# AFNO block: a chunk's moves split between SyncE's and GpSimd's queue

## The chip, the core and the metric

The kernel runs on one core of a Trainium2 chip. A core has five engines that run side by side and meet through semaphores: TensorE (matmuls; PE in the profile), VectorE (DVE), ScalarE (ACT), GpSimd (POOL) and SyncE (SP), which here only issues DMAs. DMAs can be issued by SyncE, ScalarE or GpSimd. The metric is the device time of one launch in microseconds (us), the median of several executions.

## The reference

One transformer-like block on 4096 positions of 640 channels, in float32:

```python
mod = (silu(c) @ w_mod)            # six vectors of 640: sa, ca, ga, sb, cb, gb
h = layernorm(x) * (1 + ca) + sa
x = x + ga * AFNO(h)
h = layernorm(x) * (1 + cb) + sb
x = x + gb * ((silu(h @ w_gate) * (h @ w_up)) @ w_down)

def AFNO(x):                       # 4 blocks of 160 channels
    z = rfft2(x over positions)
    h = relu(z * w1 + b1)          # complex products, block by block; relu on real and imaginary part
    o = softshrink(h * w2 + b2, 0.01)
    return irfft2(o)
```

## The kernel before, in words

The Fourier transform over 4096 positions is factored as 128 x 32 and done by matmuls with constant matrices. The AFNO stage takes some 50 to 300 us of the run, the feed-forward layer the rest.

The frequencies are worked off in 8 **chunks** (`ch`), each of which has 4 blocks of channels (`b`). One pass of the main loop is one **slot**, numbered `p = 4*ch + b`. In a slot TensorE, VectorE and ScalarE work on several chunks at once, as in a pipeline written out by hand: the first layer of slot `p` (`stage_l1`), the second stage of the forward transform for a later block (`stage_b`, `evac_b`), the second layer of slot `p - 1` (`stage_l2`), soft shrinkage of an earlier tile in four steps (`shrink_parts`, `shrink`, `shrink_high`, `shrink_low`), and the first stage of the inverse transform (`stage_i`) of slot `p - 7`. The order in which these are written in the loop is the order in which each engine gets its instructions; there is no scheduler in this stage. Every float32 matmul operand is split into a high and a low part, so most steps exist twice.

What touches the change:

- `stage_l2` writes its result with VectorE (L709) into `tts[ch, q]`, `q` = 0 and 1: two tiles of 128 partitions with real and imaginary part (`r`) beside each other. There are two `tt` buffers in all, so chunk `ch + 1` writes over those of chunk `ch`. Each slot fills one block's columns of both tiles; the first addition of a slot is for `q` = 0, the second for `q` = 1.
- When a chunk's four blocks are done (in the slot with `b == 0` of the next chunk), `move_x` copies `tt` by DMA from SBUF to SBUF into four tiles `xx`, `i` = 0 to 3: tile `i` takes the partitions `64*(i % 2)` to `64*(i % 2) + 63` of `tts[ch, i // 2]`, the real part to its lower 64 partitions, the imaginary part to its upper 64. That is eight DMAs of 64 rows of 2,560 bytes. So tiles 0 and 1 come from `q` = 0, tiles 2 and 3 from `q` = 1. `xx` has five buffers: tile 3 gets the one that tile 2 of the chunk before held, and `shrink_low` of the same slot is its last reader.
- `xx` then goes through the shrinkage, one tile in each of the following slots; `stage_i` multiplies it by a constant matrix, ScalarE copies the product to a tile `co` (two buffers, L763), and GpSimd issues the DMA that writes it to DRAM (`s2`, L764; `s<-co` in the profile).
- Behind the moves, SyncE's program has the loads of the modulation weights (`mod_load`, L531, tile `wm`), which VectorE adds up in the next slot (`mod_add`, L536 and L538), the next chunk's input (`load_g`) and, after the moves of slot 28, the load of the first rows of `x` for the layer that follows (`load_first`, L886).

The last chunk (7) isn't moved; it is shrunk and transformed in place. So there are seven handovers, in slots 4, 8, ..., 28.

Of the kernel before, what the change touches and what calls it, by code (L numbers as in the profile page):

```python
# [173 lines left out]
def body(tc, x, w1, b1, w2, b2, wg, wu, wd, c, wm, k_fa, k_tb, k_tx, k_bm, k_bx, k_ga, k_ge, k_id, out, dbg=None):  # L174
    nc = tc.nc
    pe, act, dve, pool = nc.tensor, nc.scalar, nc.vector, nc.gpsimd
# [25 lines left out]
    with ExitStack() as top:  # L202
# [35 lines left out]
        with ExitStack() as af:  # L238
# [40 lines left out]
            def weights_high(w, h, l, v, sg, eng=None):  # L279
                if eng:  # L280
                    eng.tensor_scalar(w[:, :, h], v, sg, None, op0=OP.mult)
                else:
                    act.activation(w[:, :, h], v, AF.Copy if isinstance(sg, float) else AF.Identity, scale=sg)

            def weights_low(w, h, l, v, sg):
                dve.scalar_tensor_tensor(w[:, :, l], v, sg, f32(w[:, :, h]), op0=OP.mult, op1=OP.subtract)
# [9 lines left out]
            def load_tb(ch):  # L296
                tb = lp.tile([P, 4, 128], F32, tag="tb", bufs=2, name=f"tb{ch}")
                nc.sync.dma_start(tb, k_tb[:, 4 * ch:4 * ch + 4])
                tbs[ch] = tb


            def load_g(ch, us=None):
                if ch not in gs:
                    gs[ch] = fx.tile([P, 4, D], F32, tag="gx", bufs=2, name=f"g{ch}")
                f, e = (ch, 1) if ch < 2 else (2, 2) if ch < 4 else (3, 4)
                src = s1[f].rearrange("(u v) (q e j) d -> e u (v q) (j d)", u=4, e=e, q=4)[ch % e]
                if us is None:
                    nc.sync.dma_start(gs[ch].rearrange("p j d -> p (j d)"), src.rearrange("u r d -> r u d"))
                else:
                    for u in us:  # L310
                        nc.sync.dma_start(gs[ch][u:P:4].rearrange("p j d -> p (j d)"), src[u])
# [210 lines left out]
            w, h, l, v, _ = prep2[5]  # L522
# [62 lines left out]
            tts = {}  # L585
# [4 lines left out]
            def stage_b(ch, t, tag=None):  # L590
                g, tb = gs[ch], tbs[ch]
                pb = (ps.tile([P, 2, 256], F32, tag=tag, name=f"pb{ch}_{t}") if tag else
                      bank0(1 if t == 4 else 0, [P, 2, 256], f"pb{ch}_{t}"))
                col = slice(128 * t, 128 * t + 128)
                for j in range(4):
                    mm(pb[:, :, 64 * j:64 * j + 64], g[:, j, col], tb[:, j, :], start=True, stop=True)
                pbs[ch, t] = pb

            def evac_b(ch, t):
                pb = pbs[ch, t]  # L600
                z = lp.tile([P, 2, 2, 258], F32R, tag="z", bufs=4, name=f"z{ch}_{t}")
                zs[ch, t] = z
                act.activation(z[:, 0, :, 0:256], pb, AF.Identity, scale=ca1[:, t:t + 1])
                dve.scalar_tensor_tensor(z[:, 1, :, 0:256], pb, ca1[:, t:t + 1],
                                         f32(z[:, 0, :, 0:256]), op0=OP.mult, op1=OP.subtract)
                if ch == CE:
                    pool.tensor_copy(z[:, 0, :, 0:257:256], f32(edge[:, 0, t]))
                    pool.tensor_copy(z[:, 1, :, 0:257:256], f32(edge[:, 1, t]))
                    pool.tensor_copy(z[:, :, :, 257], zero[:, 0, 0])
# [106 lines left out]

            xxs = {}

            def move_x(ch, i):
                q, h = i // 2, i % 2  # L720
                xx = p2.tile([P, D], F32, tag="xx", bufs=5, name=f"xx{ch}_{i}")
                for r in range(2):
                    nc.sync.dma_start(xx[64 * r:64 * r + 64, :], tts[ch, q][64 * h:64 * h + 64, r, :])
                xxs[ch, i] = xx


# [92 lines left out]
            def load_first_rows(lo, hi, q, e=slice(0, D)):  # L819
                for k in range(2):  # L820
                    q.dma_start(cf[k][lo:hi, :, e], s2[lo:hi, 2 * k:2 * k + 2, e])
# [4 lines left out]
            for p in range(LAST + 1):  # L826
                ch, b = p // 4, p % 4
                on(shrink, p - 6)
                on(stage_l1, p)


                if p < 4:
                    todo = ([(0, 2)], [(0, 3)], [(1, 4), (1, 0)], [(1, 1)])[p]
                elif b == 0:
                    todo = [(ch, 3)]
                else:
                    todo = [(ch + 1, 4)] * (b == 1) + [(ch + 1, b - 1)]
                todo = [q for q in todo if q[0] < NCH]
                for q in todo:
                    stage_b(*q)  # L840
                    if q[1] < 4:
                        evac_b(*q)
                for f, *a in sums.get(p, ()):
                    f(*a)

                rows = [p + 2] * (p < 4) + [p + 3] * (p > 2)
                for k in rows:
                    on(evac_rh, k)
                on(tail_l1, p)
                on(shrink_high, p - 6)  # L850
                for k in rows:
                    on(evac_rl, k)
                on(tail_low, p)
                on(stage_l2, p - 1)
                if p == 3:
                    stage_b(1, 2)
                    evac_b(1, 2)
                on(stage_i, p - 7)
                on(shrink_low, p - 6)
                if p < LAST:  # L860
                    on(shrink_parts, p - 5)
                if b == 0 and ch:
                    for i in range(4):
                        move_x(ch - 1, i)
                if p == 0:
                    for n in (3, 4):
                        weights_high(*prep2[n])
                    for job in prep2[2:5]:
                        weights_low(*job)
                if p == 0:  # L870
                    pool.dma_start(bm.rearrange("p a b c -> p (a b c)"), k_bm)
                if p == 2 or b == 3 and 2 < ch + 2 < NCH:
                    load_g(ch + 2)
                    load_tb(ch + 2)
                for f, *a in mods.get(p, ()):
                    f(*a)
                if p == LAST - 4:
                    cf += [rp.tile([P, 2, D], F32, tag=tag, name=f"cf{tag}") for tag in ("rm", "rr")]
                    load_first_rows(rb + 16, rl, nc.sync)
                elif p == LAST - 1:  # L880
                    load_first_rows(0, rb - 16, nc.sync)
# [153 lines left out]
        with ExitStack() as ff:  # L1035
# [1081 lines left out]
            for t in range(NS):  # L2117
                for n in range(NW):
                    if sum_at(n) == t:
                        a, b = sum_w(n)  # L2120
# [69 lines left out]
```

## Time and profile before

| | us |
|---|---|
| median of 3 runs | 1467.93 |
| lowest, highest | 1465.82, 1468.88 |
| the profiled execution's own time | 1467.72 |
| its span from first to last instruction | 1465.9 |

The granted TensorE clock was 0.997 in the mean. In the profile's rows a timeline line has the start, the duration, the engine, the source line, the operation and its tiles, and in brackets the idle time before it with what ended that. In a table of windows, each engine has its busy time and the number of its instructions; the last three columns are the granted clock, the mean busy share of the 16 DMA engines, and the GB/s that they moved. An `SPq` row is SyncE issuing a DMA; "to landing" is from the start of the issue to the completion semaphore. The chain of work that ended last is followed back from the last instruction to whatever released each step.

### The profile page before, as it was taken

The page shows a single profiled execution, that of the slowest core. Times are in us where ns is not written, and L with a number is a line of the kernel's source. Part 1 is how long each engine was busy: PE and PEld are TensorE (multiplying, and loading weights), DVE is VectorE, ACT ScalarE, POOL GpSimd, SP SyncE. Part 2 cuts the span into 40 slices and gives each one's busy share as a digit, 9 for nine tenths or more (in the row PEclk, how much of TensorE's full clock was granted, in tenths as well). Part 3 has the DMA queues.
Part 4 walks back from the last instruction along what each step waited for, and adds up shares of the span by engine and source line. Part 5 has one row for each costly group of instructions (what it writes and reads, how often), then busy time and mean ns, then how long its engine had stood idle before and what let it go on. Part 6 is the DMA issues. An engine that isn't in the chain of part 4 may idle for free.

```text
span 1465.9 us, 23617 instructions
## 1 busy us (share of the span) xinstructions
PE 1424.5 (97%) x8626; PEld 1344.9 (92%) x8626; DVE 1058.7 (72%) x1893; ACT 780.8 (53%) x1514; POOL 420.8 (29%) x549
## 2 busy tenths in 40 slices
PE   7899999989999999999999999999999999999998
PEld 2699999868888888899999999999999999999998
DVE  8878888888877777667777677678665566465653
ACT  7779989645445455445545455445453344344331
POOL 5500200155545244222333422434311122011111
PEclk9999999999999999999999999999999999999999
DMA  9856556667677976795766996676974446844422
GB/s 378 309 198 208 172 184 214 211 192 230 227 257 258 329 264 224 276 357 180 259 228 221 337 318 198 220 240 207 357 264 130 143 128 223 324 141 149 139 76 83
DMA packets 155223, 331.73 MB, mean 226 GB/s; under 512 B 19969, under 2 KB 79169, under 8 KB 153090
## 3 DMA queue, kind: packets, MB, share of 16 engines
q1 hardware_dynamic: 146722, 313.66, 63.0%
q0 software_dynamic: 6800, 13.93, 3.0%
q10 hardware_dynamic: 1584, 2.62, 0.5%
q8 instruction: 68, 1.11, 0.3%
q14 instruction: 49, 0.40, 0.1%
HBM read 234.35 MB, written 86.31 MB: 219 GB/s over the span
## 4 chain that ended last, share of the span: by engine, by line
PE 69%; DMA 10%; DVE 9%; ACT 5%; issue 2%; POOL 2%; SPq 2%; DVEq 0%; POOLq 0%; ACTq 0%
PE pd L2063 23%; PE pw L1868 8%; PE pw L1870 7%; PE pw L1869 7%; PE pg L1791 3%; PE pg L1792 3%; PE pg L1793 3%; DMA cr<-s 3%; PE pw L1879 2%; PE pw L1880 2%; PE pw L1881 2%; PE pc L707 2%; DMA wdr<-in_B_w_down_dram 1%; DMA wt<-td 1%; PE py L1511 1%
## 5 line engine op out<-in xcount | busy, mean ns | idle before, releaser
L2063 PE MATMUL pd<-wdh,a 128*128 128x320 f32 x1672 | 381.5, 310 | 0.5 <-DVE x L2035 0.3
L2063 PEld LDWEIGHTS pd<-wdh,a 128*128 128x128 f32 x1672 | 283.0, 188 | 1.7 <-DVE x L2035 0.7
L2063 PE MATMUL pd<-wdl,a 128*128 128x320 f32 x868 | 267.4, 309 | 0.0
L2035 DVE TENSOR_TENSOR x<-x,pd 128x320 f32<-128x320 f32 x384 | 178.2, 481 | 94.9 <-PE pd L2063 92.1
L1325 DVE TENSOR_TENSOR wb<-r,wb 128x512 fp32r<-128x512 f32 (+3 forms) x170 | 170.3, 1008 | 16.2 <-ACT wb L1318 14.9
L2063 PEld LDWEIGHTS pd<-wdl,a 128*128 128x128 f32 x868 | 163.2, 188 | 0.5
L1868 PE MATMUL pw<-h,wt 128*128 128x384 f32 x416 | 141.1, 339 | 5.0 <-DMA wt<-td 2.3
L1422 ACT ACTIVATE wdh<-wdr 128x640 fp32r<-128x640 f32 x84 | 60.8, 733 | 158.5 <-PE pd L2063 146.3
L1870 PE MATMUL pw<-h,wt 128*128 128x384 f32 x416 | 139.7, 336 | 0.0
L1869 PE MATMUL pw<-h,wt 128*128 128x384 f32 x416 | 139.5, 335 | 0.0
L1318 ACT ACTIVATE wb<-r 128x768 fp32r<-128x768 f32 (+3 forms) x168 | 115.3, 701 | 20.3 <-PE pg L1793 11.5
L1912 POOL TENSOR_TENSOR sg<-s_x,sg 128x384 f32<-128x384 f32 x24 | 26.5, 1103 | 340.0 <-DVE s_x L1894 298.4
L1868 PE MATMUL pw<-h,wb 128*128 128x384 f32 x312 | 105.0, 337 | 0.0
L1870 PE MATMUL pw<-h,wb 128*128 128x384 f32 x312 | 104.6, 335 | 0.0
L1869 PE MATMUL pw<-h,wb 128*128 128x384 f32 x312 | 104.5, 335 | 0.0
L1791 PE MATMUL pg<-ht,wb 128*128 128x512 f32 x260 | 103.7, 399 | 0.0
L1915 DVE TENSOR_TENSOR a<-sg,a 128x384 fp32r<-128x384 f32 x104 | 79.6, 769 | 32.8 <-ACT a L1914 32.5
L1792 PE MATMUL pg<-ht,wb 128*128 128x512 f32 x260 | 102.0, 392 | 0.0
L1793 PE MATMUL pg<-ht,wb 128*128 128x512 f32 x260 | 101.8, 392 | 0.0
L1426 DVE TENSOR_TENSOR wdl<-wdr,wdh 128x640 fp32r<-128x640 f32 x84 | 75.9, 913 | 27.5 <-ACT wdh L1422 27.1
L1868 PEld LDWEIGHTS pw<-h,wt 128*128 128x128 f32 x416 | 78.0, 188 | 8.1 <-ACT s_y L1887 3.9
L1494 POOL TENSOR_TENSOR cr<-cr,gab 128x640 f32<-128x640 f32 x28 | 48.5, 1734 | 116.1 <-DMA cr<-s 99.0
(276 smaller groups left out, 3370.9 us busy)
## 6 DMA issues: line engine op xcount, KB each, us to landing
wt<-td SPq DMA_DIRECT2D x104, 512.0 KB, 5.2
hs<-ho SPq DMA_DIRECT2D x52, 512.0 KB, 5.7
h<-hs SPq DMA_DIRECT2D x32, 768.0 KB, 7.3
r<-in_B_w_up_dram SPq DMA_DIRECT2D x36, 640.0 KB, 4.8
r<-in_B_w_gate_dram SPq DMA_DIRECT2D x36, 640.0 KB, 4.6
wdr<-wdd SPq DMA_DIRECT2D x35, 640.0 KB, 4.6
td<-wt SPq DMA_DIRECT2D x25, 512.0 KB, 7.1
xx<-tt SPq DMA_DIRECT2D x56, 160.0 KB, 3.4
```

Source lines behind the costliest of these rows:

```text
L1318: def high(ks, e=slice(0, c), copy=lambda o, i: act.activation(o, i, AF.Copy)):
L1325: dve.tensor_tensor(wbs[t, n][:, 1, ks, e], raw[t, n][:, ks, e], f32(wbs[t, n][:, 0, ks, e]), op=OP.subtract)
L1426: dve.tensor_tensor(l[:, f], wdraw[t, p][:, f], f32(h[:, f]), op=OP.subtract)
L1791: mm(b, wh, hh, start=(kk == 0), stop=False)
L1792: mm(b, wh, hl, start=False, stop=False)
L1793: mm(b, wl, hh, start=False, stop=(kk == 4))
L1868: mm(b, w(0, kp), a[:, kp, 0], start=start and kp == 0, stop=False, skip_group_check=not start)
L1869: mm(b, w(0, kp), a[:, kp, 1], start=False, stop=False, skip_group_check=not start)
L1870: mm(b, w(1, kp), a[:, kp, 0], start=False, stop=kp == 1, skip_group_check=not start)
L1915: Step("V", cv_ + 0.1, lambda: dve.tensor_tensor(o[:, 1], sg, f32(o[:, 0]), op=OP.subtract), (("ah", key),), ("act", t, fc, a), free=("sg" ...
L2035: dve.tensor_tensor(x2[:, e], x2[:, e], x[0][:, :320], op=OP.add)
L2063: mm(pd[g, hf][0][:, :320], l, m, start=i == 0, stop=i == len(s) - 1 and not (last and len(gs) > 1))
```

## The change

`move_x` gets the issuing engine as an argument. Tiles 0 and 1 of a chunk are still issued by SyncE, tiles 2 and 3 by GpSimd. And the call of the four moves stands directly behind `stage_l2`, ahead of `stage_i`, `shrink_low` and `shrink_parts` of the slot.

```diff
-            def move_x(ch, i):
+            def move_x(ch, i, eng=nc.sync):
                 q, h = i // 2, i % 2
                 xx = p2.tile([P, D], F32, tag="xx", bufs=5, name=f"xx{ch}_{i}")
                 for r in range(2):
-                    nc.sync.dma_start(xx[64 * r:64 * r + 64, :], tts[ch, q][64 * h:64 * h + 64, r, :])
+                    eng.dma_start(xx[64 * r:64 * r + 64, :], tts[ch, q][64 * h:64 * h + 64, r, :])
                 xxs[ch, i] = xx
...
                 on(stage_l2, p - 1)
+                if b == 0 and ch:
+                    for i in range(4):
+                        move_x(ch - 1, i, pool if i > 1 else nc.sync)
                 if p == 3:
                     stage_b(1, 2)
                     evac_b(1, 2)
...
                 on(shrink_low, p - 6)
                 if p < LAST:
                     on(shrink_parts, p - 5)
-                if b == 0 and ch:
-                    for i in range(4):
-                        move_x(ch - 1, i)
```

## The prediction

> **What bounds the kernel now.** I read the page first (busy shares and the chain that ended last), then who waits for the moves, then one handover in the timeline, then the DMA engines while moves run.
>
> ```profile
> PE 1424.5 (97%) x8626; PEld 1344.9 (92%) x8626; DVE 1058.7 (72%) x1893; ACT 780.8 (53%) x1514; POOL 420.8 (29%) x549
> PE 69%; DMA 10%; DVE 9%; ACT 5%; issue 2%; POOL 2%; SPq 2%; DVEq 0%; POOLq 0%; ACTq 0%
> xx<-tt SPq DMA_DIRECT2D x56, 160.0 KB, 3.4
> ```
>
> TensorE is busy 97% of the span, so time comes back only where TensorE itself waits, or where the chain has left it. The 56 moves are seven handovers of eight (slots 4, 8, ... 28). Who waits for them is VectorE's addition into the next chunk's `tt` (L709), which may not overwrite a buffer that a move still reads. Its rows, idle time before each in brackets:
>
> ```profile
> 100.24 0.49 DVE L709 TENSOR_TENSOR tt<-pc,b2t 128x320 f32<-128x320 f32 x1 [1.22 <-DMA xx<-tt]
> 127.79 0.49 DVE L709 TENSOR_TENSOR tt<-pc,b2t 128x320 f32<-128x320 f32 x1 [2.00 <-DMA xx<-tt]
> 157.87 0.49 DVE L709 TENSOR_TENSOR tt<-pc,b2t 128x320 f32<-128x320 f32 x1 [1.99 <-DMA xx<-tt]
> 186.69 0.49 DVE L709 TENSOR_TENSOR tt<-pc,b2t 128x320 f32<-128x320 f32 x1 [1.52 <-DMA xx<-tt]
> 217.44 0.49 DVE L709 TENSOR_TENSOR tt<-pc,b2t 128x320 f32<-128x320 f32 x1 [0.70 <-DMA xx<-tt]
> 247.38 0.49 DVE L709 TENSOR_TENSOR tt<-pc,b2t 128x320 f32<-128x320 f32 x1 [2.20 <-PE pl L670]
> 277.11 0.49 DVE L709 TENSOR_TENSOR tt<-pc,b2t 128x320 f32<-128x320 f32 x1 [1.02 <-PE pl L657]
> ```
>
> Seven waits, one at each handover, 10.65 us together. The last two name TensorE as releaser; the chain below shows moves landing just then (243.62 + 3.63, 272.74 + 4.25), so I count them as waits for moves. Each is before the second addition of its slot, the one that needs `tt[ch, 1]`: exactly the half that the change puts on another queue. What of this TensorE feels is much less:
>
> ```profile
> 131.91 0.42 PE L760 MATMUL pi<-xh,bm 128*128 128x320 f32 x1 [1.05 <-DVE u L675]
> 187.45 0.63 PE L657 MATMUL pl<-z,w1a 128*128 128x258 f32 x3 [1.02 <-DVE tt L715]
> 251.24 0.41 PE L760 MATMUL pi<-xh,bm 128*128 128x320 f32 x1 [0.25 <-DVE u L675]
> 268.38 0.41 PE L761 MATMUL pi<-xl,bm 128*128 128x320 f32 x1 [1.04 <-DVE xl L749]
> ```
>
> The first three follow the handovers of slots 8, 16 and 24: 2.32 us. The waits at 157.87 and 217.44 reach TensorE not at all. So 2 us, not 10, is the natural size of the prize.
>
> **Why a handover takes so long.** Slot 8, with the moves' landing from the chain:
>
> ```profile
> 118.89 6.00 SPq L723 DMA_DIRECT2D xx<-tt  x8
> 124.99 5.18 SPq L531 DMA_DIRECT2D wm<-in_w_mod_dram  x2
> 119.01 0.54 POOL L764 DMA_DIRECT2D s<-co  x1 [6.40 <-ACT co L763]
> 119.17 0.81 DVE L749 TENSOR_TENSOR xl<-xx,xh 128x640 fp32r<-128x640 f32 x1
> 125.29 0.49 DVE L709 TENSOR_TENSOR tt<-pc,b2t 128x320 f32<-128x320 f32 x1
> ...
> 124.29 3.41 DMA xx<-tt
> 243.62 3.63 DMA xx<-tt
> 272.74 4.25 DMA xx<-tt
> ```
>
> SyncE needs 6.00 us to issue eight moves, and the last lands at 127.70, 8.81 us after the first issue. The issue looks like the limit. But the windows over the moves (the last two columns are DMA share and GB/s) say that the DMA engines are full:
>
> ```profile
> 120.00:127.70 7.70, 7.70 (x64) 7.70 (x63) 5.28 (x10) 7.58 (x18) 0.54 (x1) 1.00 0.95 252
> 121.00:122.00 1.00, 1.00 (x10) 1.00 (x9) 1.00 (x3) 0.98 (x4) 0.00 (x0) 1.00 1.00 320
> ...
> s<-co POOLq DMA_DIRECT2D x28, 320.0 KB, 3.7
> wm<-in_w_mod_dram SPq DMA_DIRECT2D x20, 320.0 KB, 3.0
> x<-in_A_x_dram SPq DMA_DIRECT2D x1, 1280.0 KB, 8.7
> ```
>
> Ahead of the last landing lie eight moves of 160 KB and the 320 KB of `s<-co`, issued at 119.01: 1.64 MB, at 252 GB/s 6.5 us. The remaining 8.81 - 6.5 = 2.3 us are start and completion. So faster issue alone brings little; what counts is which bytes stand ahead of the second half.
>
> **The change part by part.** *Moved to GpSimd's queue*: 28 of the 56 moves, four in each handover. The instruction order of the two built kernels shows four fewer on SyncE, four more on GpSimd, the rest of SyncE's order as it was, and unchanged orders on TensorE, VectorE and ScalarE. GpSimd's price for issuing, from its other DMAs:
>
> ```profile
> L316 POOL DMA_DIRECT2D g<-xa x4: 572/584/797, 47.9 to 50.2; - x4
> DMA to landing us min/median/max: 3.4/3.6/4.0
> ...
> L764 POOL DMA_DIRECT2D s<-co x28: 539/542/591, 112.0 to 293.9; - x28
> ```
>
> L316 is SBUF to SBUF, as the moves are: 4 x 0.58 = 2.3 us. The two on the first tile can start when the second addition of slot 8 ends (about 119.3). The two on the last tile reuse the buffer that `shrink_low` (L749) still reads, to 119.98; SyncE had the same wait, but reached it late. The last issue starts near 121.2, against 124.29 before. GpSimd is otherwise idle here (6.40 us before L764), so the issue itself is hidden.
>
> *Placed behind the second layer*: on SyncE nothing lies between the old place and the new, so there this moves nothing. On GpSimd the four moves pass the same slot's write `s<-co`, which leaves some 2 to 3 us later and behind 640 KB. Cover: `co` has two buffers, so ScalarE wants this one two slots later, about 13.8 us (27.55 us from the L709 row of slot 4 to that of slot 8, half of it). Without the cover ScalarE's L763 would stall for up to those 3 us; slot 28 is the thin place (below).
>
> *SyncE is free 3.0 us earlier* (half of the 6.00): the next load in its order, `wm` (320 KB), now enters right behind the first half and competes with the second. Of the bytes ahead of the last landing, 320 KB of `s<-co` go behind and up to 320 KB of `wm` come in. Bounds: all of `wm` ahead, 0 us earlier; none ahead, 320 KB / 252 GB/s = 1.3 us earlier; and if two queues together keep the 320 GB/s of the window at 121, the eight moves take 4.1 + 2.3 us = 6.4, which ends the wait. I take queues served alike: both halves drain together, `wm` meets only the rest by which GpSimd started later (about half a move, 0.3 us): 1.0 us earlier.
>
> Stall by stall: slot 8 2.00 to 1.0, slot 16 1.52 to 0.5, slot 24 2.20 to 1.2. TensorE's 1.05, 1.02 and 0.25 lose 1.0, 1.0 and 0.25: 2.25 us. Slots 12 and 20: 0, they were covered. Next late after this: the matmuls themselves. Slot 4 has no `s<-co` ahead that could go behind, so there `wm` is pure addition, but VectorE wants that load next:
>
> ```profile
> 101.14 0.55 DVE L536 TENSOR_SCALAR acc<-wm,sc 128x640 f32<-128x640 f32 x1 [0.41 <-DMA wm<-in_w_mod_dram]
> ```
>
> At worst its 1.3 us less these 0.41, at best 0.41 gained; I take 0.2 us lost.
>
> Slot 28 is different:
>
> ```profile
> 267.27 6.67 SPq L723 DMA_DIRECT2D xx<-tt  x8
> 274.05 0.94 SPq L886 DMA_DIRECT2D x<-in_A_x_dram  x1
> 276.53 0.77 ACT L763 ACTIVATE co<-pi 128x320 f32<-128x320 f32 x2
> 267.61 0.54 POOL L764 DMA_DIRECT2D s<-co  x1 [6.71 <-ACT co L763]
> ...
> 277.11 0.49 DVE tt L709
> ```
>
> Here SyncE's next is a load of 1280 KB, which now starts some 3.3 us sooner (half of 6.67), beside the second half; and ScalarE's `co` at 276.53 needs the buffer of the write at 267.61, which now goes behind the moves. Bounds: 1.02 us gained (the wait at 277.11 gone), or 2.6 us lost (third rival). I take 0: less ahead from `s<-co`, more from the load.
>
> Sum: -2.25 + 0.2 + 0 = -2.05 us. The profiled execution took 1467.72 us (span 1465.9), beside the median of 1467.93, so no offset is needed: **1465.7 us**. Behind slot 28 all work follows the AFNO stage and shifts with it; FFN orders are fixed.
>
> **Rivals.** *No gain* (1467.7): the DMA engines carry the same bytes, and `wm` takes the place of `s<-co` in full. For it: the 0.95 share above. Against: the order of bytes does change. The Trainium skill, "DMA: Bandwidth & Descriptors", section "Issuing engines are not separate DMA queues", states this as a rule: DMAs from several engines run on the same 16 DMA engines, and issuing from several saves only issue time. By that rule, with the engines full, the gain is nil; the trace agrees on the full engines.
>
> *All of it* (1463.5): two queues run at the 320 GB/s and the waits vanish. Then TensorE regains 2.32, slot 28 another 1.02, and the 1.04 at 268.38, where VectorE is behind, goes too: up to 4.4, 1463.3; I name 1463.5. Against: the move-only rate of 252 may be the moves' own.
>
> *Slower* (1470.9): at slot 28 the 1280 KB load gets ahead of the second half. Net of one or two `s<-co` of 320 KB that fall behind, 640 to 960 KB more at 252 GB/s: 2.6 to 3.9 us later at 277.11, which is itself a piece of the chain (the last row above) and passes it on; `wm` cancels the gains elsewhere. It decides from the point at which over half the load lands first; below that slot 28 costs under 1 us. For it: the load's rows are 10,240 bytes, the moves' 2,560. The Trainium skill, same page, section "Queues, rings and completion order", says that each DMA engine takes turns between queues by packets; with packets of a row each the load would get four bytes for one, and by that this rival would be the case. No view of this profile shows the turns.
>
> That the change does not do what it says is excluded by the instruction order.
>
> **How the numbers follow.** Forecast 0.38, all of it 0.24, no gain 0.20, slower 0.18. A measurement of this kernel can tell about 0.2% (2.9 us; the three runs spread over 3.06). Faster by more, below 1465.0: 0.24 and a quarter of the forecast, 0.34. Slower by more, above 1470.8: somewhat over half of its rival, and a little for a GpSimd issue that costs twice 0.58, 0.13. Within: 0.53. The range goes from 1463.0, which keeps most of the best case, to 1469.8, which cuts off most of the slower one.
>
> **What would show it.** Right: the second additions at slots 8, 16, 24 wait about 1 us or less, TensorE's rows at 131.91 and 187.45 lose their idle time, GpSimd's L723 takes 0.5 to 0.7 us each. No gain: the last move still lands 8.8 us after the first issue. Slower: at slot 28 L709 or L763 waits 2 us and more for DMA. Wrong altogether: first additions, which need the first half, begin to wait for as long as the second ones did.

## The result, and the profile after

The changed kernel takes 1475.94 us (median of six runs, 1474.24 to 1478.44), the kernel before on the same chip 1468.36 (six runs, 1463.11 to 1469.46): a ratio of 1.0061, 95% interval 1.0042 to 1.0079. It is slower by 7.6 us where 2 us less were forecast. The profiled execution took 1475.19 us, its span is 1473.4, the granted clock 0.995.

The additions into `tt` (L709) still wait for moves, but others than before, and longer. First the answer on this line (duration ns min/median/max; what ended its idle time and who waited for it, us and times), then slot 8 in the timeline, then the pieces of the chain of waits at slots 8 and 24:

```profile
L709 DVE TENSOR_TENSOR tt<-pc,b2t x64: 479/484/492, 72.5 to 307.2; 128x320 f32<-128x320 f32 x64
...
  DMA xx<-tt: 19.1, 6
  PE pl L670: 3.4, 1
...
  POOL xx L723: 51.4, 6
  PEld pc L707: 5.2, 6
  PE pc L707: 4.0, 5
```

```profile
121.49 0.89 DVE L709 TENSOR_TENSOR tt<-pc,b2t 128x320 f32<-128x320 f32 x2
122.01 4.00 SPq L723 DMA_DIRECT2D xx<-tt  x4
122.68 2.06 POOL L723 DMA_DIRECT2D xx<-tt  x4 [6.96 <-DVE tt L709]
124.73 0.58 POOL L764 DMA_DIRECT2D s<-co  x1
132.10 0.89 DVE L709 TENSOR_TENSOR tt<-pc,b2t 128x320 f32<-128x320 f32 x2 [3.84 <-DMA xx<-tt]
```

```profile
124.10 7.92 DMA xx<-tt
...
249.26 8.31 DMA xx<-tt
```

The two additions of a slot now run back to back (x2, 0.89 us), and the wait of 3.84 us stands ahead of the first. Before, the first began 6.41 us after SyncE's first move and waited for nothing; the second waited 2.00. Now the first begins at 132.10, 10.09 us after it. The seven waits are 2.66, 3.84, 3.41, 3.47, 3.02, 4.02 and 2.11 us: 22.5 together, where the second additions had 10.65. (The 3.41, of slot 12, stands under TensorE in the rows above; but the matmuls named there had ended 0.7 us before the addition began, so I count it as a wait for moves.) The chain names what is waited for: SyncE's fourth move, issued at 124.10, lands at 132.02. GpSimd issues its four in 2.06 us, from 122.68, as forecast, and they are down 1.9 us before that one. So the half that stayed on SyncE, and was issued first, lands last.

Who waits at TensorE, in the waits by line from 91 to 315 us (us in total, times, longest), before and after; the rows left out are alike on both sides, the largest being 2.1 us for `xl` in both:

```profile
PE pi L760 <- DVE u L675: 1.3, 2, 1.1
PE pl L657 <- DVE tt L715: 1.0, 1, 1.0
```

```profile
PE pc L707 <- DVE tt L709: 4.0, 5, 1.4
PE pi L760 <- DVE u L675: 3.1, 5, 0.9
PE pl L657 <- DVE tt L715: 2.8, 1, 2.8
```

2.3 us have become 9.9. The difference of 7.6 is as large as that of the medians (1475.94 - 1468.36 = 7.58). As these are single executions, the match to the tenth is partly luck: from the first move of slot 4 to that of slot 28 they differ by 8.4 us (174.7 and 183.0). New is the first row: the next matmuls of the second layer wait for the late additions, which still hold their PSUM tiles.

The DMA engines moved no more per second than before (252 GB/s). The windows over the moves of slots 8 and 16, DMA share and GB/s last:

```profile
123.00:132.00 9.00, 8.20 (x66) 8.01 (x64) 4.91 (x10) 8.83 (x21) 2.85 (x6) 1.00 0.95 242
185.00:194.00 9.00, 7.45 (x59) 7.02 (x57) 4.38 (x9) 8.06 (x18) 2.92 (x6) 1.00 0.96 241
```

The page's queue lines (packets, MB, share), before and after, tell what a move is made of on each queue:

```profile
q1 hardware_dynamic: 146722, 313.66, 63.0%
q0 software_dynamic: 6800, 13.93, 3.0%
```

```profile
q1 hardware_dynamic: 144482, 309.07, 61.7%
q0 software_dynamic: 8144, 18.52, 4.6%
```

28 moves left q1 (SyncE) and took 2,240 packets with them: 80 each, 64 rows of 2,560 bytes and 16 to signal completion. On q0 (GpSimd) they are 1,344: 48 each, so 32 for the same data, of 5,120 bytes. GpSimd's packets hold two rows.

Both queues' packets, with the small ones that signal completion, from 125 to 130 us, in the middle of slot 8's moves of after:

```profile
q0 software_dynamic: 208, 0.72, 63.6%
q1 hardware_dynamic: 201, 0.42, 35.5%
```

The two queues moved nearly the same number of packets, and so GpSimd's moved 0.72 MB where SyncE's moved 0.42.

### The profile page after: what moved, and what is told of

Read it like the earlier page. It is cut to its first block, busy times and chain, and to the rows that moved or that the text cites. A ratio compares the mean times of both kernels' runs of the same rounds, so it can differ in the third digit from the quotient of the medians.

```text
span 1473.4 us, 23638 instructions
## 1 busy us (share of the span) xinstructions
PE 1426.9 (97%) x8626; PEld 1347.0 (91%) x8626; DVE 1058.4 (72%) x1893; ACT 780.7 (53%) x1514; POOL 432.2 (29%) x577
## 4 chain that ended last, share of the span: by engine, by line
PE 69%; DMA 11%; DVE 10%; ACT 4%; issue 3%; POOL 2%; SPq 1%; DVEq 0%; POOLq 0%; ACTq 0%
PE pd L2063 22%; PE pw L1868 7%; PE pw L1870 7%; PE pw L1869 7%; DMA xx<-tt 4%; PE pg L1791 3%; PE pg L1792 3%; PE pg L1793 3%; DMA cr<-s 2%; PE pw L1879 2%; PE pw L1881 2%; PE pw L1880 2%; PE pc L707 2%; DVE wb L1325 1%; PE py L1511 1%
```

## Experiments

The theories: **turns by packets** (the queues share the DMA engines packet by packet, so the first half loses its precedence, and against GpSimd's two-row packets it gets less than its share of bytes); **ports** (two queues that copy between the same partition halves hold each other up); **place** (the new place in the loop costs).

### The parts of the change by themselves

All moves on SyncE at the new place:

```diff
-                        move_x(ch - 1, i, pool if i > 1 else nc.sync)
+                        move_x(ch - 1, i)
```

> The new place alone: all eight moves stay on SyncE. Theory 1 (turns): GpSimd's queue carries packets of two rows (5,120 bytes), SyncE's of one (2,560), the DMA engines take turns by packets, so the half on SyncE's queue is served last. Theory 2 (ports): two queues that copy between the same halves of the partitions slow each other, the rate falls. Theory 3 (place): issuing the moves at the new place is what costs. SyncE's order is the same as before the change, so theories 1 and 2 expect the time of before, 1468 within 2 us, first additions without a wait, second additions 0.7 to 2.2 us; theory 3 expects 1474 and more.

1465.80 us against 1468.82, ratio 0.9986 (0.9968 to 1.0003). Every engine has its instructions in the order of before; first additions wait for nothing, second ones 0.7 to 2.3 us. The place by itself costs nothing that shows.

The two queues at the old place, so that GpSimd's moves come behind the slot's `s<-co`:

```diff
                 on(stage_l2, p - 1)
-                if b == 0 and ch:
-                    for i in range(4):
-                        move_x(ch - 1, i, pool if i > 1 else nc.sync)
...
                     on(shrink_parts, p - 5)
+                if b == 0 and ch:
+                    for i in range(4):
+                        move_x(ch - 1, i, pool if i > 1 else nc.sync)
```

> The other part alone: the second half on GpSimd, at the old place, behind the slot's write of co. Theory 1: that write (also two rows a packet) now goes ahead of the second half, the half on SyncE is still served last: first additions wait 2 to 4 us as in the changed kernel, time 1473 to 1477. Theory 2: the same time, two queues still run together. Theory 3: 1468.

1471.90 us, ratio 1.0024 (1.0002 to 1.0046). The first additions wait 2.65, 2.78, 1.13, 2.52, 1.62, 2.79 and 1.17 us, 14.7 together. That is a little less than any of the theories of two queues expected (1473 to 1477, waits of 2 to 4 us), and the interval is only just clear of 1. Still, the second queue alone costs; and since the place alone costs nothing, what it adds in the change comes with the moves passing the write.

The halves exchanged:

```diff
-                        move_x(ch - 1, i, pool if i > 1 else nc.sync)
+                        move_x(ch - 1, i, pool if i < 2 else nc.sync)
```

> The changed kernel with the halves exchanged: first half on GpSimd, second on SyncE. Theory 1: the half on SyncE lands last whichever tiles it has: first additions wait under 1 us, second additions take the wait, 2 to 4 us, the last SyncE move lands 9.5 to 10 us after the first issue; time 1473 to 1477. Theory 2: both halves late alike, first additions wait 2 us and more here too.

1482.84 us, ratio 1.0099 (1.0065 to 1.0134). From the waits by line:

```profile
DVE tt L709 <- DMA xx<-tt: 19.8, 12, 3.1
...
DVE tt L709 <- PE pl L657: 3.7, 2, 2.2
```

Fourteen waits, two of them put down to TensorE: both additions of each handover wait. GpSimd's half, now the first, lands 7 to 9 us after the first issue, too late as well (first additions wait 0.7 to 2.2, where under 1 was expected, and the time is above the 1473 to 1477 of that theory), and SyncE's half again lands last, from slot 8 on at 10 to 11.6 (second additions wait up to 3.1). It is SyncE's half that comes last, whichever it is, as turns by packets expected; that the first half is late too only ports had foreseen, though with both halves late alike, which they are not.

SyncE's four moves in reverse order, so that the queues use opposite partition halves at any time:

```diff
+                for eng, i, r in ((nc.sync, 1, 1), (pool, 2, 0), (nc.sync, 1, 0), (pool, 2, 1),
+                                  (nc.sync, 0, 1), (pool, 3, 0), (nc.sync, 0, 0), (pool, 3, 1)):
+                    q, h = i // 2, i % 2
+                    eng.dma_start(xxs[ch, i][64 * r:64 * r + 64, :], tts[ch, q][64 * h:64 * h + 64, r, :])
```

> The changed kernel with the order of SyncE's four moves turned round, so that at any time the two queues read from, and write to, opposite halves of the 128 partitions. Theory 1: order within a queue changes nothing, first additions wait 2 to 4 us, 1474 to 1478. Theory 2: the two queues stop hindering each other, the DMA rate over the moves rises from about 242 to 320 GB/s and more, all moves land by 7.5 us after the first issue, the waits fall under 1 us, 1464 to 1467.

1479.79 us, ratio 1.0078 (1.0047 to 1.0109). All moves are down at 8.3 to 9.7 us, a little sooner than after, and yet it is no faster. A new wait explains part of that:

```profile
DVE tt L709 <- DMA xx<-tt: 12.7, 5, 3.4
ACT cl L730 <- DMA xx<-tt: 12.2, 6, 3.2
```

Tile 0 is now moved last, and ScalarE's shrinkage (L730) wants it first. Neither theory's figures came: the moves were to land by 7.5 us with ports, and the order was to change nothing with turns. But the sharing changed. In five us of slot 16, from 3 us after the first move, SyncE's queue had 275 packets to GpSimd's 176, where after had 180 to 203. So one packet for one isn't what the queues get in every arrangement, and the run doesn't decide on ports.

GpSimd's moves in column halves, rows of 1,280 bytes:

```diff
-                    eng.dma_start(xx[64 * r:64 * r + 64, :], tts[ch, q][64 * h:64 * h + 64, r, :])
+                    for e in ((slice(0, 320), slice(320, 640)) if eng is pool else (slice(0, 640),)):
+                        eng.dma_start(xx[64 * r:64 * r + 64, e], tts[ch, q][64 * h:64 * h + 64, r, e])
```

> After, with each of GpSimd's moves cut into two column halves (rows of 1,280 bytes, twice the issues: 8 x 0.52 = 4.2 us at a handover). Turns by packets: if its packets still hold two rows, they are now as long as SyncE's; SyncE's half ends 1 to 1.5 us sooner than in after, the first additions wait 22.5 us less 7 to 10, and the time is 1471 to 1474. If its packets grow to four rows, nothing changes. Ports: SyncE's half ends as late as in after, first additions wait 20 to 23 us, 1475 to 1477.

```profile
q0 software_dynamic: 8592, 18.52, 4.3%
```

448 packets more than after: 16 for each added DMA, no more for data. The packets stayed at 5,120 bytes, now four rows, and by the branch written for that nothing should change: 1478.27 us, ratio 1.0068 (1.0046 to 1.0090), is after's. But it isn't a clean test: the narrow moves need only half the columns of `tt`, and GpSimd's first one left 0.2 to 12 us ahead of SyncE's. Inconclusive.

### The moves by themselves

Kernels without the computation. The first of them let its handovers run into one another, and the writes left at the start:

> Leaves out the whole computation: x is copied through to the output, and then handovers are made by themselves, three times over, each begun only when the one before has landed whole. Eight moves of 160 KB all on SyncE; half on SyncE and half on GpSimd; half on SyncE and half on ScalarE; SyncE and GpSimd with opposite source halves, then with opposite destination halves; SyncE and GpSimd with a 320 KB write behind GpSimd's, and with it ahead; all on SyncE with that write; GpSimd's moves in two column halves each; four moves on SyncE alone; four on GpSimd alone. Turns by packets (GpSimd's hold two rows, SyncE's one): all on SyncE ends 7.4 us after the first issue, as at slot 4 of before; SyncE's half beside GpSimd's ends last, at 8.4 as at slot 4 of after, and with the write behind GpSimd's at 9.5 to 10; beside ScalarE's (one row as well) both halves end together by 7.5; opposite halves change nothing; with column halves SyncE's part ends at 7.5 or sooner. Ports (two queues between the same partition halves hold each other up): SyncE and ScalarE end at 8.4 and later too, opposite halves bring both back to 7.5 or sooner, and column halves change nothing.

Nothing is read from it. In the second a single VectorE instruction (L192) over the one buffer that holds all tiles stands between the handovers:

```diff
+        def ready():
+            dve.memset(al[:, :, 0:1], 2.0)
...
+            ready()
+            for j in range(4):
+                sync.dma_start(*pair(j))
+                pool.dma_start(*pair(j + 4))
+            pool.dma_start(s2[k], co)
```

> Leaves out the whole computation, as the first one of moves alone; now all tiles lie in one buffer, and one VectorE instruction over the whole of it stands between the handovers, so that each begins only when the one before has landed whole. Turns by packets (GpSimd's of two rows, SyncE's and ScalarE's of one): eight moves on SyncE end 7.4 us after the first issue; SyncE's half beside GpSimd's ends last, at 8.4; with the 320 KB write behind GpSimd's at 9.5 to 10; beside ScalarE's both halves end together by 7.5; opposite source or destination halves change nothing against the same halves. Ports: SyncE beside ScalarE ends at 8.4 or later too, and opposite halves bring SyncE beside GpSimd back to 7.5 or sooner. Four moves on SyncE alone end by 4.9 in both.

The timeline of VectorE, third time round. The idle time of each row is the handover that stands before it: all on SyncE; SyncE and GpSimd; SyncE and ScalarE; opposite sources; opposite destinations; the write behind GpSimd's moves; the write ahead of them; the write and all on SyncE; (column halves left out); SyncE's four alone; GpSimd's four alone:

```profile
226.74 0.07 DVE L192 MEMSET al<- 128x9 f32 x1 [7.37 <-DMA al<-al]
234.83 0.07 DVE L192 MEMSET al<- 128x9 f32 x1 [8.03 <-DMA al<-al]
243.17 0.07 DVE L192 MEMSET al<- 128x9 f32 x1 [8.27 <-DMA al<-al]
251.01 0.07 DVE L192 MEMSET al<- 128x9 f32 x1 [7.78 <-DMA al<-al]
258.89 0.07 DVE L192 MEMSET al<- 128x9 f32 x1 [7.82 <-DMA al<-al]
268.29 0.07 DVE L192 MEMSET al<- 128x9 f32 x1 [9.33 <-DMA al<-al]
277.08 0.07 DVE L192 MEMSET al<- 128x9 f32 x1 [8.73 <-DMA al<-al]
286.07 0.07 DVE L192 MEMSET al<- 128x9 f32 x1 [8.92 <-DMA al<-al]
...
297.95 0.07 DVE L192 MEMSET al<- 128x9 f32 x1 [4.99 <-DMA al<-al]
303.01 0.07 DVE L192 MEMSET al<- 128x9 f32 x1 [4.99 <-DMA al<-al]
```

Two queues bring nothing for the whole (7.37 against 8.03 and 8.27), and four moves alone take as long on either queue (4.99). When each half is down, from the landings of the same handovers, us from the first issue:

| handover | first half | second half | write |
|---|---|---|---|
| all on SyncE | 4.7 | 7.2 | |
| SyncE, GpSimd | 7.8 | 7.3 | |
| SyncE, ScalarE | 7.7 | 7.9 | |
| SyncE, GpSimd, opposite sources | 7.6 | 7.2 | |
| SyncE, GpSimd, opposite destinations | 7.6 | 7.2 | |
| SyncE, GpSimd, write behind GpSimd's | 9.1 | 8.0 | 8.8 |
| SyncE, GpSimd, write ahead of GpSimd's | 8.5 | 8.3 | 4.4 |
| all on SyncE, write on GpSimd | 5.9 | 8.4 | 4.4 |

This is the case in small. On one queue the first half is down at 4.7, because the second stands behind it. On two, whichever the second is, it is down only with the second, 3 us later. Opposite halves change 0.2 us: for the moves by themselves ports are out. (No run had opposite halves with the write behind them, as the reversed order above has.) With opposite sources SyncE's fourth issue took 0.6 us in place of 1.6, and its half came only those 0.2 us sooner, so the long issue isn't what holds it up. Turns by packets had a miss here: SyncE's half was to be down at 8.4 beside GpSimd's two-row packets and by 7.5 beside ScalarE's; without the write there is no such difference (7.8 and 7.7). The 320 KB behind GpSimd's moves add 1.3 us more, to the half on the *other* queue.

Whether the size of the packets decides that last piece, or the bytes on the second queue alone (one of five handovers):

```diff
+            for j in range(4):
+                sync.dma_start(*pair(j))
+                act.dma_start(*pair(j + 4))
+            act.dma_start(s2[4 + k], co)
```

> Leaves out the whole computation, as the other runs of moves alone. Four moves on SyncE beside four on a second queue, and a 320 KB write behind one of the queues: GpSimd's moves and GpSimd's write (the case of after); ScalarE's moves and ScalarE's write; ScalarE's moves, the write on GpSimd; GpSimd's moves, the write on ScalarE; GpSimd's moves, the write behind SyncE's own. Packet size (GpSimd's packets hold two rows and take more bytes at each turn): SyncE's half ends last of all, at 9.2 us after the first issue, only where GpSimd's queue carries moves and write; behind ScalarE's moves and write, with equal packets, SyncE has its half by 8.0 to 8.2, when each queue has moved the same bytes, and ScalarE's write ends after it at 9. With three queues at work SyncE's half ends between. Number of bytes alone (whatever stands on the other queue goes first): 9.2 with ScalarE's queue too.

VectorE's rows for GpSimd's moves with GpSimd's write, and for ScalarE's moves with ScalarE's write, second and third time:

```profile
109.03 0.07 DVE L192 MEMSET al<- 128x9 f32 x1 [9.57 <-DMA al<-al]
118.76 0.07 DVE L192 MEMSET al<- 128x9 f32 x1 [9.67 <-DMA s<-al]
...
156.22 0.07 DVE L192 MEMSET al<- 128x9 f32 x1 [9.59 <-DMA al<-al]
166.08 0.07 DVE L192 MEMSET al<- 128x9 f32 x1 [9.79 <-DMA s<-al]
```

The whole takes the same time, but another ends last: beside GpSimd a move on SyncE (9.2 to 9.3, the write 8.9 to 9.0), beside ScalarE the write (9.2 to 9.4), with SyncE's half down at 8.2 to 8.5. That is what turns by packets gave. The queues' packets in the second time round show it too, in the 4.5 us from 2.5 us after the first issue (101.99 to 106.49 beside GpSimd, 111.62 to 116.12 beside ScalarE):

```profile
q0 software_dynamic: 189, 0.66, 64.8%
q1 hardware_dynamic: 162, 0.33, 34.1%
...
q10 hardware_dynamic: 249, 0.50, 53.2%
q1 hardware_dynamic: 230, 0.49, 47.5%
```

In both, the two queues moved packets in like number; SyncE's (q1) moved half of GpSimd's bytes, and as many as ScalarE's. These are sums over 4.5 us: single turns aren't seen. ScalarE's moves have 80 packets each, as SyncE's, by the queue line of the run before this one (12 moves):

```profile
q10 hardware_dynamic: 960, 1.97, 2.9%
```

Of the 1.3 us that the write adds beside GpSimd (7.8 to 9.1), 0.5 to 0.8 are there beside ScalarE too (7.7 to 8.2 and 8.5); the rest, about half, goes with GpSimd's queue, by the rows above with the size of its packets. ScalarE's write left only 3.8 us after the first issue, GpSimd's at 2.3, so the comparison is not quite even. In the three handovers not shown, with the write on a third queue or behind SyncE's own moves, SyncE's half is down at 8.4 to 8.6, between the two.

### The write behind the moves, and a third buffer

After, with the write of slots 8 to 24 issued only behind the next slot's:

```diff
-                pool.dma_start(s2[4 * J:4 * J + 4].rearrange("k n d -> (k n) d"), co)
+                late.append((J, co))
+                if i != 1 or 4 * ch + i > 20:
+                    for j, c in late[::-1]:
+                        pool.dma_start(s2[4 * j:4 * j + 4].rearrange("k n d -> (k n) d"), c)
+                    late.clear()
```

> After, with the write s<-co of handover slots 8 to 24 issued only behind the next slot's, so that 320 KB less follow GpSimd's moves. Turns by packets: this write shares GpSimd's turns and holds back SyncE's half; without it SyncE's half ends 1.3 us sooner (320 KB at 250 GB/s), first additions wait about 6 us less in all, and the time is 1472 to 1474. Ports: the write touches neither half's destination, the waits stay within 1 us of after's 22.5 in sum, 1475 to 1477.

```profile
DVE tt L709 <- DMA xx<-tt: 9.0, 4, 2.6
DVE tt L709 <- PE pl L657: 5.9, 3, 2.6
```

1469.21 us, ratio 1.0011 (0.9993 to 1.0029), 6.7 below after: more than expected. SyncE's half is down at 8.3 to 9.7 us in slots 8 to 24, the first additions wait 14.9 in all (the two rows; the second is put down to TensorE, at the same additions) instead of 22.5.

The same edit made to before:

> Before, with the write s<-co of handover slots 8 to 24 issued only behind the next slot's; all moves on SyncE as before. If bytes ahead of the second half are what counts: its last move lands 1 to 1.3 us sooner at those slots, second additions wait 1.2 to 2.0 us less each, TensorE's 1.05 and 1.02 us behind slots 8 and 16 go, and the time is 1466 to 1467 (2 us less than before). If the queue's own pace counts, or the two writes of the next slot come in the way: no change, 1468.5, or up to 2 us more.

1464.53 us, ratio 0.9977 (0.9961 to 0.9992), 3.6 below before where 2 were expected, though the waits of second additions in slots 8 to 24 fell by only 0.2 to 1.3 us each. In slots 16 to 24 the second half is down at 7.4 to 7.6 us (before 8.4 to 8.8), and TensorE's 1.05 us behind slot 8 and 1.02 behind slot 16 have shrunk to one of 0.7, beside another 0.7 for ScalarE's `xh`.

Before, with three buffers for `tt`, so that the second additions too write over what the *first* half of the moves reads:

```diff
-                r2 = hp.tile([P, 258], F32R, tag="r2", bufs=4, name=f"r2_{ch}_{b}")
+                r2 = hp.tile([P, 258], F32R, tag="r2", bufs=2, name=f"r2_{ch}_{b}")
...
-                        tts[ch, q] = p2.tile([P, 2, D], F32, tag="tt", bufs=2, name=f"tt{ch}_{q}")
+                        tts[ch, q] = p2.tile([P, 2, D], F32, tag="tt", bufs=3, name=f"tt{ch}_{q}")
```

> Before, with three buffers for tt in place of two (and two for r2 in place of four, to make room): the second additions of a handover slot then write a buffer that only the first four moves read. If the waits for the second half are what a handover costs: the seven waits of second additions (10.65 us) go, TensorE's 2.3 us behind slots 8, 16 and 24 with them, and the time is 1464.5 to 1466.5. If r2 with two buffers makes its writers wait, it is 1470 or more.

1481.01 us, ratio 1.0089 (1.0067 to 1.0110). The waits at the handovers are gone, but the waits by line from 55 to 112 us have two that before has not:

```profile
POOL w2a L281 <- DMA s<-xa: 27.3, 1, 27.3
...
PE pl L657 <- ACT h L661: 18.2, 1, 18.2
```

The larger pool shifted `w2a` onto a buffer that was still being written out; TensorE stood 18.2 us in the first slot. With the later write and with the change this stays:

> Three buffers for tt (two for r2) and the deferred write s<-co together, all moves on SyncE. If the write costs only by holding up the second half, nothing is left for it to bring: the same as with three buffers alone, within 1 us. If the bytes count elsewhere as well (the additions of s<-co beside loads), up to 3 us less than that.

> After, with three buffers for tt (two for r2): the second additions of a slot then wait for SyncE's half of the moves, the first ones for GpSimd's half of the handover before it, long landed. If the whole cost of the change is that the first additions wait for a half that lands late: second additions wait instead, first ones not, they stand some 0.4 us further on in VectorE's order, and most of the 7.6 us stays (1471 to 1475). If the cost lay in the issue on GpSimd or in the writes of s<-co that go late: about 1475, with the waits for moves as they are.

1481.51 us (1.0089, 1.0064 to 1.0115) and 1493.46 (1.0173, 1.0148 to 1.0198). In the second, the wait went to the second additions (2.14 to 3.56 us each) as expected: three buffers don't help a half that lands late, since it is the first half that all of them need. The split costs 12.4 us here (1493.46 less 1481.01), more than its 7.6 with two buffers; between slots 4 and 28 the profiled executions differ by 9.6, and where the rest lies isn't shown.

With the third buffer at the low end of the pool, so that `w2a` stays where it was, and then with the later write as well:

```diff
+            ty = [p2.tile([P, 2, D], F32, tag="ty", bufs=1, name="tt1_0")]
             acc = p2.tile([P, D], F32, name="acc")
```

> Before, with a third buffer for tt (two for r2) as in the earlier run, but laid at the low end of its pool, so that w2a and all other tiles of the pool stay where they are in before. If the 18.2 us that TensorE waited in the first slot of that run came only from w2a lying on a buffer still being written out: they go, the 2.2 us between the handovers of slots 4 and 28 and their end stay gained, 1465 to 1466.5. If r2 with two buffers is what cost the time: 1475 or more.

> The same with the write s<-co of handover slots 8 to 24 issued behind the next slot's. If the write costs only by holding up the second half: as the run without it, within 1 us. If it also costs elsewhere: up to 1.5 us less (from slot 4's first move to slot 28's it was 171.9 us with three buffers and the later write, 173.1 with three buffers alone, 172.5 with the later write alone, 174.7 before).

1464.62 us, ratio 0.9981 (0.9964 to 0.9999), and 1462.90, ratio **0.9966 (0.9950 to 0.9981)**, the fastest of all, though these two intervals overlap. No addition waits for a move in either.

The runs that tell the queues, the write and the third buffer apart (those with the shifted `w2a` left out) in order, each with its ratio to the kernel before, measured beside it (1467.5 to 1468.8). "TensorE" is the sum of its three kinds of wait shown above, "4 to 28" the time from the first move of slot 4 to that of slot 28, both from the profiled execution:

| moves | write `s<-co` | us | ratio | TensorE | 4 to 28 |
|---|---|---|---|---|---|
| one queue, 3 buffers | later | 1462.90 | 0.9966 | 1.4 | 172.7 |
| one queue | later | 1464.53 | 0.9977 | 0.7 | 172.5 |
| one queue, 3 buffers | ahead | 1464.62 | 0.9981 | 1.0 | 172.8 |
| one queue (before) | ahead | 1468.36 | 1 | 2.3 | 174.7 |
| two queues | later | 1469.21 | 1.0011 | 4.0 | 176.4 |
| two queues | ahead | 1471.90 | 1.0024 | 4.5 | 178.8 |
| two queues (after) | behind | 1475.94 | 1.0061 | 9.9 | 183.0 |

The second queue costs 3 to 5 us at either place of the write (1471.90 less 1468.82, 1469.21 less 1464.53), and the write directly behind the moves another 4 to 7 (1475.94 less 1471.90 and 1469.21). One execution's waits don't give the last two us of a median: the feed-forward layer, which holds none of this, varied by up to 6 us between these executions (1143.4 to 1149.0 from its first `w_gate` matmul to the end).

## Why the prediction was wrong, point by point

- **The step that failed**: "I take queues served alike: both halves drain together". The sum drew from it what the *second* half gains and nothing for the first, though halves that drain together also end together. It left out 3 us for the first half, which had its place by standing first in a single queue. The sign on that is plain: the first additions could run from 5.9 to 8.3 us after the first issue, the single queue had the half down at 4.8 in slot 4 and 5.7 in slot 16, and everywhere ahead of the fifth move, which landed at 5.5 to 6.9; the two queues had it down at 8.4 to 10.5. The prediction named it, as the case in which it is "wrong altogether", and gave it no price and no chance.
- **The write**: it was counted as bytes that leave the path of the second half. They do, and join the path of the first. Ahead 1471.90, behind 1475.94, later 1469.21. This term had the wrong sign.
- **Right, but beside the point**: the second half was to land about 1.0 us sooner; it did by 0.7 at slot 8 (8.81 to 8.15), 0.5 at 16 and 0.9 at 24. GpSimd's issues cost 0.52 us each (2.06 for four), and the place by itself moved nothing. The DMA engines were full, and two queues gave no more (242 GB/s).
- **SyncE free 3.0 us sooner**: 2.0 at slot 8. Its four issues take 4.00 us there, where 588 ns is the median for one and 1,915 the longest:

```profile
L723 SPq DMA_DIRECT2D xx<-tt x28: 469/588/1915, 94.9 to 280.1; - x28
```

- **Stall by stall**: slots 8, 16 and 24 were to give back 2.25 us; slots 12 and 20, put at 0 as covered, now stop TensorE for 1.0 and 0.7. The cover held for a second addition 2.0 and 0.7 us late, not for both of them 3.4 and 3.0 late.
- **The rivals**: *no gain* and *all of it* fell, both on the wrong side. *Slower* had the sign by another mechanism: at slot 28 the 1280 KB load stands behind SyncE's half, and GpSimd's half was down at 7.9 us, ahead of it; the first addition waits 2.11 us, the least of the seven. ScalarE's wait for `co` is there, 1.1 us once.
- **The Trainium skill**, "DMA: Bandwidth & Descriptors": the section "Queues, rings and completion order" has the DMA engines take turns between queues by packets. With the write behind the moves the runs agree in the mean: packets of both queues in like number, and SyncE's half ends before or after the same 320 KB according to whether the other queue's packets hold one row or two. The reversed order (275 to 176) does not. The prediction saw the rule only for the load of slot 28, not for the moves. The section "Issuing engines are not separate DMA queues" says that a second issuing engine saves only issue time. On bandwidth the runs agree (7.37 us on one queue, 8.03 on two). But it isn't all: the split took the order away, which cost 3 to 5 us here.

Still open: how much of the 4 to 7 us of the write behind the moves is packet size alone, in the whole kernel, since no run had other packets on GpSimd's queue; and the reversed order, where SyncE's queue gets a larger share and the moves land sooner than after, without a gain.

## What to carry to other kernels

A single DMA queue was also an order here: of eight moves by themselves on it the first four were down at 4.7 us and the last at 7.2. Before transfers are spread over two queues, ask which of them is needed first, and price its loss of precedence; with the DMA engines full, the one half gained 0.5 to 0.9 us here and the other lost some 3 or more. And what stands behind a transfer on its own queue can hold up transfers on the other: the bulk write was better issued a slot later than beside the moves on one queue (0.23%), or than right behind them on two (1469.21 against 1475.94).

## What was not expected of the hardware

GpSimd's queue made packets of 5,120 bytes of rows of 2,560, and of 1,280 too, where SyncE's packets had one row each (80 packets for a 160 KB move, against 48). Beside it SyncE's 640 KB landed after GpSimd's 960 KB that were issued with it (9.1 against 8.8 us); beside ScalarE's queue it was the other way round (8.2 to 8.5, and 9.2 to 9.4).
